# Loading most of the third group's k and v ahead of its transposable blocks on SP's queue

## The chip, the cores and the metric

The kernel runs on one core of a Trainium2 chip. The metric is the device time of one launch in microseconds (us), as the median over several runs. A core has a matrix engine (PE, with its weight loads shown apart as PEld), three engines for elementwise work (DVE, ACT, POOL), and a queue engine SP that does no arithmetic and only issues transfers. POOL issues transfers as well. All engines run their own instruction lists in order and wait for each other through semaphores.

## The reference, cut to what matters

Lightning attention over blocks of the sequence, with a decaying state per head, and then a two-layer network whose activation is h - tanh(h):

```python
# batch 4, heads 8, sequence 768, head size 64; lam: one decay per head
intra = einsum('bhic,bhjc->bhij', qb, kb) * Dmask        # scores within a block
intra = einsum('bhij,bhjd->bhid', intra, vb)
inter = einsum('bhid,bhde->bhie', qb * lam_pow, kv_state) # what came before the block
out   = intra + inter
kv_state = lam_block * kv_state + einsum('bhsd,bhse->bhde', kb * rev_pow, vb)
# bridge to x: 3072 tokens x 512
h = x @ w_in          # 512 x 2048
g = h - tanh(h)
y = g @ w_out         # 2048 x 512
```

## The kernel before, in words

**Tiling.** The sequence of 768 is cut into six groups of 128 positions (g = 0 to 5), and each group has one chunk for each of the four batches (b = 0 to 3). "The third group" is g = 2. Group 0 goes through a plain network (`up_plain`, `down_plain`), groups 1 to 5 through a network whose products are split by Strassen's scheme into seven (n = 1 to 7), and five of those seven are split once more into seven on the way down (`down_twice`, L536; x names the inner product). While the network of group g runs, the attention of group g + 1 is done in pieces between its products: `p0` for chunks 0 and 1, `p1` for chunks 2 and 3, each made of `att_transpose` (L275), `att_scores` (L296), `att_out` (L332) and `att_state` (L310).

**Two forms of the inputs.** For g of 2 and above (`GB = 2`) a chunk is loaded in two forms. The natural form, `k_nat` and `v_nat` (`load_natural`, L122, transfer at L127), has positions on partitions; one transfer of 256 KB each. `att_state` scales `k_nat` on DVE in place (L318) and multiplies it with `v_nat` on PE (L323); `att_out` multiplies `v_nat` with the scores on PE (L354). The block form, `q_blk` and `k_blk` (`load_blocks`, L132, transfers at L140), is sixteen transfers of 16 KB for each of q and k; DVE turns a block tile with one stream transpose into `qt` or `kt` (L283).

**Buffers.** `k_nat` has three buffers, `v_nat` four (L123, L124), used in turn by all groups. So k of chunk (2, 0) takes the buffer of (1, 1), k of (2, 1) that of (1, 2), k of (2, 2) that of (1, 3), and k of (2, 3) that of (2, 0); v of (2, b) takes that of (1, b). The buffers of group 1 come free with its `att_state`, one call for chunks 0 and 1 and one for chunks 2 and 3. The block tiles have seven buffers (L649), in memory that stages weights until `early.close()` (L648); the eighth block tile of a group, k of chunk 3, takes the buffer of the first and waits for its transpose.

**What sets the order.** All loads of the third group are issued by SP, in the order of `load` (L143 to L165), because `keep_in_program_order` holds the L127 and L140 transfers of g >= 2 to the order in which the program names them. Before the change that order is: blocks of q and k for chunks 0, 1, 2, the blocks of q for chunk 3 (seven tiles, 112 transfers), natural k and v of chunks 0 and 1, the k blocks of chunk 3, natural k and v of chunks 2 and 3. The same order is used for groups 3, 4 and (with v alone) 5. The main loop (L656 to L696) sets where the attention pieces stand among the products on PE: `down(g, 2)`, then `p0[2:]` (`att_out`, `att_state` of chunks 0 and 1), then `down_twice` with n = 4, the transposes of chunks 2 and 3 (`p1[0:1]`), `down_twice` with n = 5, the scores of chunks 2 and 3, and so on.

**Weights of the way down.** They lie in device memory (`factors`, `fine`) and come through a ring of seven buffers `wb` (`piece`, L472), loaded from POOL at L479 and L482. Results go out from POOL at L490.

Of the kernel before, what the change touches and what calls it, by code (L numbers as in the profile page):

```python
# [17 lines left out]
GB = 2  # L18
# [5 lines left out]
def kernel(  # L24
# [97 lines left out]
    def load_natural(g, b, names):  # L122
        for name, src, bufs in (("q", q, 2), ("v", v, 4), ("k", k, 3)) if (g, b) == (0, B - 1) else (  # L123
                ("q", q, 2), ("k", k, 3), ("v", v, 4)):  # L124
            if name in names:
                x = (qpool if name == "q" else io).tile([128, H, D], F32, name=f"{name}_nat", tag=name, bufs=bufs)
                op = nc.sync.dma_start(out=x, in_=src[b, :, ts(g, BLK), :].rearrange("h s d -> s h d"))  # L127
                if g >= GB:
                    tc.keep_in_program_order(op)
                raw[g, b][name] = x  # L130

    def load_blocks(g, b, names):  # L132
        for name, src in (("q", q), ("k", k)):
            if name in names:
                x = late["blk"].tile([128, NP, BLK // 32, 32], F32, name=f"{name}_blk", tag="blk")
                for p in range(NP):
                    for c in range(4):
                        blk = src[b, 2 * p + c // 2, ts(g, BLK), ts(c % 2, 32)]
                        tc.keep_in_program_order(
                            nc.sync.dma_start(out=x[ts(c, 32), p], in_=blk.rearrange("(r t) a -> t r a", t=32)))  # L140
                raw[g, b][name + "b"] = x

    def load(n):  # L143

        while at["loaded"] < min(n, len(chunks)):
            g, b = chunks[at["loaded"]]
            if g < GB:
                raw[g, b] = {}  # L150
                load_natural(g, b, "qkv")
                at["loaded"] += 1
                continue
            for b in range(B):
                raw[g, b] = {}
            nat = "kv" if g < NG - 1 else "v"
            for b in range(B - 1):
                load_blocks(g, b, "qk")
            load_blocks(g, 3, "q")
            for b in (0, 1):  # L160
                load_natural(g, b, nat)
            load_blocks(g, 3, "k")
            for b in (2, 3):
                load_natural(g, b, nat)
            at["loaded"] += B  # L165


# [93 lines left out]


    load(B)
    load_weights(WAHEAD)

# [9 lines left out]
    def att_transpose(g, bs):  # L275
        for b in bs:
            load(g * B + b + 1)
            t = raw[g, b]
            qt = work.tile([128, NP, BLK], F32, name="qt", tag="qt")
            kt = work.tile([128, NP, BLK], F32, name="kt", tag="kt")  # L280
            for dst, x in ((qt, "q"), (kt, "k")):
                if g >= GB:
                    tc.keep_in_program_order(nc.vector.transpose(out=dst.rearrange("d p i -> d (p i)"),  # L283
                                                                 in_=t[x + "b"].rearrange("d p r a -> d (p r a)")))
                else:
                    tp = bank("tp", "att", 4).rearrange("d (p s) -> d p s", p=NP)
                    for p in range(NP):
                        nc.tensor.transpose(out=tp[:, p, :], in_=t[x][:, 2 * p:2 * p + 2, :], identity=ident)
                    nc.scalar.activation(dst, tp, AF.Copy)
            qd = None  # L290
            if g > 0:
                qd = work.tile([128, NP, BLK], F32, name="qd", tag="qd")
                nc.vector.tensor_tensor(qd, qt, fwd, op=AL.mult)
            tr[g, b] = (qt, kt, qd)
# [432 lines left out]
```

## Time and profile before

| what | value |
|---|---|
| median of 4 runs | 690.72 us (686.94 to 694.71) |
| the profiled execution | 690.78 us, its span 689.0 us |
| PE busy | 665.7 us, 97% of the span |
| PEld, DVE, ACT, POOL busy | 575.9, 449.7, 194.3, 188.5 us |
| DMA | 123.27 MB, mean 179 GB/s |
| transfers of natural v, natural k (L127) | 24 and 20, 256 KB each, median 5.1 and 4.7 us to landing |
| transfers of blocks of q and of k (L140) | 256 and 256, 16 KB each, median 3.5 and 3.4 us to landing |
| `wb` from `fine`, from `factors` (POOL) | 168 and 44, 256 KB each, median 4.2 and 5.4 us to landing |

The span is the time from the first to the last recorded instruction of the one profiled execution; its own time is 1.78 us longer. A timeline row gives the start, the time, the engine and line, what is written and read, the number of instructions merged, and in brackets the idle time before it and what ended it. A row of stages gives the length of a stretch and each engine's busy time in it; PEclk is the share of full clock that PE was granted there.

### The profile page before, as it was taken

The numbers are of one execution on the slowest core, as the hardware profiler recorded it, in microseconds if no ns is written. First come the engines' busy times: TensorE is split into PE (matmuls) and PEld (weight loads), VectorE is DVE, ScalarE is ACT, GpSimd is POOL, SyncE is SP. The second block draws the span as 40 slices with busy tenths as digits, with TensorE's granted clock in tenths as the row PEclk, the third lists the DMA queues.
The fourth block names the chain that finished last, engine by engine and source line by source line (L and its number), as shares of the span: only waits on it lengthen the run. The fifth ranks groups of instructions, "written<-read, shape, count | busy, mean of one in ns | idle before, by whom it ended". The sixth has DMA issues, their size and how long they took to land.

```text
span 689.0 us, 12449 instructions
## 1 busy us (share of the span) xinstructions
PE 665.7 (97%) x4688; PEld 575.9 (84%) x4688; DVE 449.7 (65%) x786; ACT 194.3 (28%) x392; POOL 188.5 (27%) x325
## 2 busy tenths in 40 slices
PE   6899999999998789999999999999999999999998
PEld 5688855558887689888899888899988899988887
DVE  3798767992995775447885447777356776254743
ACT  2664433322321112332112332112233122233120
POOL 0001424227652245001254100144200244300352
PEclk9999999999999899999999999999999999999999
DMA  9869878639988898426498542498630576400485
GB/s 189 216 212 248 266 234 273 209 100 282 295 252 236 182 292 225 115 39 131 130 290 240 144 85 47 130 278 234 192 56 10 144 237 206 170 1 0 122 277 168
DMA packets 160427, 123.27 MB, mean 179 GB/s; under 512 B 133488, under 2 KB 133872, under 8 KB 160368
## 3 DMA queue, kind: packets, MB, share of 16 engines
q0 software_dynamic: 27504, 91.77, 41.9%
q1 hardware_dynamic: 132720, 30.71, 23.1%
q8 instruction: 37, 0.61, 0.4%
q14 instruction: 22, 0.18, 0.1%
q10 hardware_dynamic: 144, 0.00, 0.0%
HBM read 99.62 MB, written 22.81 MB: 178 GB/s over the span
## 4 chain that ended last, share of the span: by engine, by line
PE 87%; DMA 6%; issue 4%; POOL 2%; ACT 0%; DVE 0%; SPq 0%; POOLq 0%
PE y L405 20%; PE z L405 10%; PE y L548 10%; PE h L590 8%; PE op L606 8%; PE zw L548 7%; PE w L510 5%; PE w L405 5%; PE y L510 5%; PE sp L303 3%; DMA wb<-fine 3%; PE op L354 2%; POOL wb L479 1%; DMA wb<-factors 1%; PE op L348 1%
## 5 line engine op out<-in xcount | busy, mean ns | idle before, releaser
L479 POOL DMA_DIRECT2D wb<-fine x168 | 90.7, 540 | 143.1 <-PE y L548 56.9
L482 POOL DMA_DIRECT2D wb<-factors x44 | 24.0, 546 | 188.8 <-PE y L510 176.9
L405 PE MATMUL y<-xt,w 128*128 128x256 f32 x320 | 73.2, 379 | 0.0
L405 PEld LDWEIGHTS y<-xt,w 128*128 128x128 f32 x320 | 60.5, 190 | 8.5 <-issue 0.5
L413 ACT ACTIVATE th<-g 128x512 f32<-128x512 f32 x60 | 37.7, 630 | 93.1 <-DVE g L431 41.7
L551 ACT ACTIVATE q<-y 128x128 f32<-128x128 f32 x96 | 26.7, 278 | 124.0 <-PE y L548 123.1
L548 PE MATMUL y<-wb,g 128*128 128x128 f32 x456 | 61.3, 278 | 0.0
L414 DVE TENSOR_TENSOR g<-g,th 128x512 f32<-128x512 f32 x60 | 41.4, 689 | 27.5 <-ACT th L413 27.2
L548 PEld LDWEIGHTS y<-wb,g 128*128 128x128 f32 x456 | 55.7, 192 | 1.5 <-issue 0.3
L606 PE MATMUL op<-wt,g 128*128 128x512 f32 x128 | 56.5, 595 | 0.0
L590 PE MATMUL h<-xt,w 128*128 128x256 f32 x256 | 56.1, 381 | 0.0
L590 PEld LDWEIGHTS h<-xt,w 128*128 128x128 f32 x256 | 48.3, 190 | 7.3 <-issue 0.3
L606 PEld LDWEIGHTS op<-wt,g 128*128 128x128 f32 x128 | 23.8, 190 | 27.7 <-issue 26.5
L426 DVE TENSOR_TENSOR g<-g,z 128x512 f32<-128x512 f32 x20 | 13.7, 685 | 44.4 <-ACT g L425 44.4
L548 PE MATMUL zw<-wb,g 128*128 128x128 f32 x304 | 40.1, 275 | 0.0
L405 PE MATMUL z<-tt,ws 128*128 128x256 f32 x160 | 37.9, 380 | 0.0
L405 PE MATMUL y<-tt,w 128*128 128x256 f32 x160 | 37.9, 380 | 0.0
L405 PE MATMUL w<-xt,w 128*128 128x256 f32 x160 | 37.8, 379 | 0.0
L405 PE MATMUL y<-tt,ws 128*128 128x256 f32 x160 | 37.8, 379 | 0.0
L405 PE MATMUL z<-xt,ws 128*128 128x256 f32 x160 | 37.8, 379 | 0.0
L307 DVE TENSOR_TENSOR ss<-sp,mask 128x512 f32<-128x512 f32 x48 | 30.8, 682 | 10.7 <-PE sp L303 10.7
L548 PEld LDWEIGHTS zw<-wb,g 128*128 128x128 f32 x304 | 37.0, 192 | 0.0
(125 smaller groups left out, 1219.3 us busy)
## 6 DMA issues: line engine op xcount, KB each, us to landing
wb<-fine POOLq DMA_DIRECT2D x168, 256.0 KB, 4.2
wb<-factors POOLq DMA_DIRECT2D x44, 256.0 KB, 5.4
raw<-in_moe_w_out_dram POOLq DMA_DIRECT2D x16, 512.0 KB, 5.1
v_nat<-in_v_dram SPq DMA_DIRECT2D x24, 256.0 KB, 5.1
factors<-wt POOLq DMA_DIRECT2D x8, 768.0 KB, 5.5
k_nat<-in_k_dram SPq DMA_DIRECT2D x20, 256.0 KB, 4.7
raw<-in_moe_w_in_dram SPq DMA_DIRECT2D x8, 512.0 KB, 5.2
raw<-in_moe_w_in_dram SPq DMA_DIRECT2D x16, 256.0 KB, 5.1
```

Of the source, the lines that this page charges most:

```text
L303: nc.tensor.matmul(out=sp[j][:, p, :], lhsT=kt[ts(j, 64), p, :], rhs=qt[ts(j, 64), p, :], start=True, stop=True)
L307: nc.vector.tensor_tensor(ss[:, j], sp[j], mask[:, j], op=AL.mult)
L405: nc.tensor.matmul(out=t[:, m, :], lhsT=wt[:, kt, ts(m, 128)], rhs=x[:, kt, :], start=first and m == 0 and kt == 0, stop=kt == 1, skip_gro ...
L413: nc.scalar.activation(th, src, AF.Tanh)
L414: nc.vector.tensor_tensor(dst(c), src, th, op=AL.subtract)
L479: nc.gpsimd.dma_start(out=t.rearrange("p m c -> p (m c)"), in_=fine[TWICE.index(n_), SUB.index(x_)].rearrange("p u c -> p (u c)"))
L482: nc.gpsimd.dma_start(out=t, in_=factors[XAT[FACT[n_][1]]][:, 2 * x_:2 * x_ + 2, :])
L510: nc.tensor.matmul(out=t[:, m, :], lhsT=a[:, u, kt, ts(m, 128)], rhs=wb[:, kt, :], start=first and u == 0 and m == 0 and kt == 0, stop=u = ...
L548: nc.tensor.matmul(out=dst, lhsT=a[:, u, :], rhs=wb[:, ts(u, 128)], start=x in (1, 2) and u == 0, stop=u == NU - 1, skip_group_check=True)
L551: nc.scalar.activation(keep, dst, AF.Copy)
L590: nc.tensor.matmul(out=hm[:, m, :], lhsT=w1[u][:, i, a, ts(m, 128)], rhs=xt[0, t][:, i, :], start=m == 0 and i == 0, stop=i == KI - 1, ski ...
L606: nc.tensor.matmul(out=obank[b], lhsT=g, rhs=wt[:, 2 * a:2 * a + 2, :], start=kt == 0 and a == 0, stop=kt == KH - 1 and a == 1)
```

## The change

For the third group alone (g == GB), k and v of chunks 0, 1 and 2 in natural form are issued before any of the group's blocks. Their old places, before and after the k blocks of chunk 3, are left out for that group; natural k and v of chunk 3 stay behind those blocks. Six transfers move; none is added or taken away, and no other group changes.

```diff
@@ -154,14 +154,20 @@
             for b in range(B):
                 raw[g, b] = {}
             nat = "kv" if g < NG - 1 else "v"
+
+            first = (0, 1, 2) if g == GB else ()
+            for b in first:
+                load_natural(g, b, nat)
             for b in range(B - 1):
                 load_blocks(g, b, "qk")
             load_blocks(g, 3, "q")
             for b in (0, 1):
-                load_natural(g, b, nat)
+                if b not in first:
+                    load_natural(g, b, nat)
             load_blocks(g, 3, "k")
             for b in (2, 3):
-                load_natural(g, b, nat)
+                if b not in first:
+                    load_natural(g, b, nat)
             at["loaded"] += B
```

## The prediction

> **What bounds the kernel now.** I read the page first: PE is busy for 97% of the span, so time can be won only where PE stands idle. Then I asked for the waits, and for busy time by stage. The first three rows below run from the start of `att_out` of chunks 0 and 1 to the first product of `down_twice` n = 4, for g = 2, 3 and 4; the last three from there to the scores of chunks 2 and 3, for g = 2, 3 and 5. The work in each set is alike but for g = 5, which has no state to update.
>
> ```profile
> 220.20:232.96 12.76, 5.46 (x97) 4.77 (x97) 6.10 (x10) 1.09 (x2) 1.29 (x2) 0.73 0.75 153
> 337.36:341.22 3.86, 3.86 (x97) 3.62 (x97) 3.86 (x8) 1.08 (x2) 1.26 (x2) 1.00 0.41 136
> 443.19:447.05 3.86, 3.86 (x97) 3.62 (x96) 3.86 (x7) 1.09 (x2) 1.26 (x2) 1.00 0.34 127
> 232.96:248.01 15.05, 13.11 (x117) 12.80 (x114) 10.78 (x19) 2.50 (x9) 7.04 (x13) 1.00 0.97 263
> 341.22:353.92 12.70, 12.70 (x114) 12.58 (x114) 11.32 (x21) 2.50 (x9) 5.96 (x11) 1.00 1.03 282
> 553.00:565.70 12.70, 12.70 (x114) 12.58 (x114) 10.08 (x19) 3.19 (x11) 7.49 (x14) 1.00 0.76 243
> ```
>
> The third group loses 12.76 - 3.86 = 8.90 us in the first stretch and 15.05 - 12.70 = 2.35 us in the second. The timeline names what ends the first idle time:
>
> ```profile
> 223.44 0.39 SPq L127 DMA_DIRECT2D k_nat<-in_k_dram  x1
> 223.87 0.58 SPq L127 DMA_DIRECT2D v_nat<-in_v_dram  x1
> ...
> 226.55 5.61 SPq L140 DMA_DIRECT2D k_blk<-in_k_dram  x10
> 226.74 0.69 DVE L318 TENSOR_TENSOR k_nat<-k_nat,mask 128x512 f32<-128x512 f32 x1 [7.98 <-DMA k_nat<-in_k_dram]
> ...
> 227.94 1.98 PE L354 MATMUL op<-ss,v_nat 128*64 128x128 f32 x16 [6.64 <-DMA v_nat<-in_v_dram]
> ```
>
> SP reaches natural k and v of chunk 0 only at 223.44, when PE is already at `att_out`; DVE stands 7.98 us, PE 6.64. Why so late? SP's own timeline has it in 112 block transfers without a pause from 144.86 to 223.4. What it did before that, the waits of SP between 105 and 146 us say:
>
> ```profile
> SPq L127 <- PE kv L323: 18.9, 1, 18.9
> SPq L140 <- DMA raw<-in_moe_w_out_dram: 16.4, 2, 8.6
> SPq L140 <- DVE wt L260: 15.9, 1, 15.9
> ```
>
> After its last L127 transfer of group 1 (issued at 111.94) SP sat for some 32 us until the staging memory was free for the blocks: 16.4 + 15.9. That gap is where the six moved transfers go. The second stretch:
>
> ```profile
> 241.38 0.67 DVE L283 STREAM_TRANSPOSE kt<-k_blk 128x512 f32<-128x512 f32 x1
> ...
> 241.97 0.65 DVE L293 TENSOR_TENSOR qd<-qt,fwd 128x512 f32<-128x512 f32 x1
> 242.54 0.68 DVE L553 TENSOR_TENSOR gS<-gS,s 128x512 f32<-128x512 f32 x1
> 243.21 1.13 PE L548 MATMUL y<-wb,s 128*128 128x128 f32 x8 [1.94 <-DMA wb<-fine]
> ...
> 246.06 1.06 PE L548 MATMUL zw<-wb,gS 128*128 128x128 f32 x8
> ```
>
> PE waits 1.94 us for a weight piece, while SP's naturals of chunks 2 and 3 (235.17 to 239.4) share the DMA engines with it. The reader should also see the order on DVE: the transpose of chunk 3's k (241.38) stands ahead of L553, and L553 feeds the product at 246.06 (n = 5, x = 3).
>
> **What the Trainium skill says.** "DMA: Bandwidth & Descriptors", section "Anatomy of one DMA — SWDGE (gpsimd) path": a semaphore wait is served by the issuing sequencer before dispatch, not by the DMA engines. So a load that waits for its buffer holds everything behind it on SP; the trace agrees (18.9 us in one wait). Same page, "Issuing engines are not separate DMA queues": transfers of SP and POOL run on the same 16 engines, so moving one saves no transfer time; the trace agrees, the DMA share is 0.97 in the stretch where PE waits for `wb`. "TensorE: Matmul & The Clock Gate", "Part 1: The HAM clock gate": after an idle window of about 3.4 us PE falls to half clock. The trace agrees in kind: PEclk is 0.73 over the first stretch, against 1.00 in its like. That slow clock lies inside the 8.90 us; I don't add it.
>
> **The change, part by part.**
>
> *Moved to the front.* Natural k and v of chunk (2, 0) find their buffers free when `att_state` of group 1's chunks 0 and 1 ends (PE L323, 111.27 + 1.10 = 112.37): issued at about 112.4. Next is k of (2, 1), which must wait for k of (1, 2), read by the L323 that runs 139.86 to 140.96. Behind that wait on SP stand only v(2, 1), k and v(2, 2) and the blocks, and the blocks can't start before 144.8 in any case. Four naturals in a row took SP 226.44 - 223.44 = 3.0 us; from 140.5 or 141 they end by 144.0. So SP reaches the blocks on time.
>
> *Who else is disturbed.* k of (1, 3), issued at 111.94 and needed at 120.58, is ahead of the new pair on the queue; the weight loads of POOL at 112 and 114 share the engines with it. The waits between 105 and 150 us show no instruction waiting for `raw`; its users wait for PE. Cost 0 under that cover; without it, up to one landing, some 5 us.
>
> *Blocks pushed back.* The four naturals issued at 141 to 144 are still moving when the blocks begin. Bounds: 0 (the DMA share from 140 to 150 us is 0.49, so there is room for them) and 7.2 us (the four naturals of 223.44 took until 230.59, when their last consumer starts). I take d = 1 us: the blocks' 0.47 us each at the start is SP's own issue rate, and only the last natural or two are still out.
>
> *Removed from their old places.* Behind the seventh block tile (223.4 + d) SP goes straight to k blocks of chunk 3; the two pairs that stood before them took 3.0 us.
>
> *The stall.* Naturals in place since about 149, `att_out` and `att_state` run at 220.20 as for g = 3 and 4: -8.90 us. DVE's L318 no longer holds L532, L533 and L519, and POOL's store of L519 no longer holds the weight pieces (it waited 10.22 us).
>
> *What is late next.* Everything on PE and DVE shifts 8.90 us earlier, but SP's k blocks of chunk 3 shift only 3.0 - d = 2 us. DVE now wants them at 241.38 - 8.90 = 232.48. They are issued from 224.4; a tile's sixteen take 7.5 us at best (several rows), 8.53 here before, 10.5 at 201.43; I take 8.5 and a landing of 3.0 (medians by window: 2.0 to 5.0). Landing L = 223.4 + 1 + 8.5 + 3.0 = 235.9. From that transpose's start to the end of L553 is 242.54 + 0.68 - 241.38 = 1.84 us, with the hand-over 2.0: the product x = 3 starts at 237.9. Undisturbed it would start at 224.06 + 12.70 - 1.88 = 234.88 (1.88 is 247.94 - 246.06, from x = 3 to the scores). Loss 3.0 us. Bounds on L: 223.4 + 0 + 7.5 + 2.0 = 232.9 (loss 0), and 223.4 + 7.2 + 10.5 + 5.0 = 246.1 (loss 13.2, which is 2.0 us slower than before).
>
> *The weight wait.* Half of the naturals that shared its window are gone, and while PE waits for x = 3 the ring of seven fills: -2.35 us for the second stretch, in place of which stands the 3.0.
>
> *Later.* k and v of chunk (2, 3) follow at about 233 and land near 240; they are needed at 254.85 - 8.2. Group 3's blocks start some 5 us sooner; its naturals, issued at 308 to 311, are used at 337. So nothing downstream can undo the shift: PE is without a gap from 267 to 373.
>
> **Sum:** -8.90 - 2.35 + 3.0 = -8.2 us, against the profiled 690.78: 682.6. That execution is within 0.1 us of the median, so the same number stands for it. The four runs spread over 7.8 us.
>
> **The rivals.**
> 1. *Blocks in time.* L under 234, no new wait: the whole 11.25, 679.5 us. For it: the best block rate seen, 7.5 us. Against: weight pieces run at the same moment.
> 2. *Blocks later.* L of 239 to 242: x = 3 at 241 to 244, loss 6 to 9, 686 to 689. For it: block tiles took 10 to 13 us in the busy stretch from 164 to 223. Against: the two kinds of load met at 342.19 with 9.23 us a tile.
> 3. *Another wait in its place, or no move.* The weight ring, used 8.9 us sooner, waits as long as the naturals did, or the loads stay late because their buffer waits don't clear when I say: 689 to 691. Against: g = 3 and 5 run this stretch without a gap, g = 4 with 0.49 us.
> 4. *Slower.* Naturals and blocks pass one after the other: four landings of 4.9 us put the stream 19.6 us back, L = 254.5, x = 3 at 256.5, 10.4 us behind before: 701. It turns into a loss from L = 244.1 and reaches 1% at 251.0. Against: four naturals together took 7.2 us, not 19.6.
>
> **How the numbers follow.** One per cent is 6.9 us, about what a measurement can tell from no change; 683.8 corresponds to L = 237. Forecast (L from 234 to 238, 681 to 685): 0.55, of it 0.45 below 683.8. Rival 1: 0.12. Rival 2: 0.15. Rival 3: 0.08. Rival 4: 0.10. Faster 0.45 + 0.12 = 0.57; same 0.10 + 0.15 + 0.08 = 0.33; slower 0.10. The range from 678.5 to 690.0 takes in the forecast, rivals 1 and 2 and part of 3.
>
> **What would show it.** Right: L127 rows at about 112.4 and 140.5 to 144; blocks from about 145; no wait of L354 or L318 for a natural; the first stretch 3.9 us long; a DVE wait of about 3 us for `k_blk` before the last transpose, with x = 3 after it. Wrong: blocks starting after 147, a wait for `wb` over 2 us in `down_twice` n = 4 or 5, a PE gap before 155, or instructions of DVE in another order around the transposes.

## The result, and the profile after

The changed kernel takes 688.53 us (median of 43 runs, 684.70 to 691.55) against 690.8 us for the kernel before (64 runs): 0.9967 of its time, 95% interval 0.9956 to 0.9979. That is 2.3 us less, where 8.2 us less was forecast. Line numbers behind `load` are six higher from here on than in the kernel before: L289 is the stream transpose, L309 the scores, L324 the scaling of `k_nat`, L554 and L559 the products and the DVE step of `down_twice`.

The profiled execution (688.0 us span) has the two stretches of the forecast again, and a third from the product x = 3 of n = 5 to the first product of n = 6:

```profile
221.11:224.97 3.86, 3.86 (x97) 3.62 (x96) 3.86 (x7) 1.09 (x2) 1.29 (x2) 1.00 0.55 157
224.97:248.19 23.22, 14.94 (x117) 14.36 (x113) 11.76 (x21) 2.50 (x9) 7.04 (x13) 0.80 0.78 200
244.50:250.70 6.20, 6.20 (x49) 5.85 (x49) 3.21 (x7) 0.28 (x1) 1.08 (x2) 0.61 0.40 96
```

The first stretch is exactly what it is in the groups that never waited: 12.76 us became 3.86. The second grew from 15.05 to 23.22, and the clock column shows 0.80 in it and 0.61 in the third, which overlaps its end. The stall was handed on. The timeline of DVE and PE says to whom:

```profile
235.37 1.06 PE L554 MATMUL y<-wb,gS 128*128 128x128 f32 x8
...
242.51 0.71 DVE L289 STREAM_TRANSPOSE kt<-k_blk 128x512 f32<-128x512 f32 x1 [8.84 <-DMA k_nat<-in_k_dram]
243.15 0.65 DVE L299 TENSOR_TENSOR qd<-qt,fwd 128x512 f32<-128x512 f32 x1
243.72 0.68 DVE L559 TENSOR_TENSOR gS<-gS,s 128x512 f32<-128x512 f32 x1
...
244.50 2.05 PE L554 MATMUL zw<-wb,gS 128*128 128x128 f32 x8 [8.08 <-issue]
246.34 1.91 PE L554 MATMUL y<-wb,gS 128*128 128x128 f32 x8
248.19 2.58 PE L309 MATMUL sp<-qt,kt 64*128 64x128 f32 x32
```

DVE stands 8.84 us before the transpose of chunk 3's k. L559 is two places behind it, and the product that starts at 244.50 needs L559; PE stands 8.08 us. A row of eight like instructions took 1.06 us at 235.37 and 2.05 us after the pause. "issue" in PE's bracket means that the profile names no releaser; the times of L559 give it. SP's timeline shows why the blocks came so late:

```profile
141.16 0.37 SPq L127 DMA_DIRECT2D k_nat<-in_k_dram  x1
141.58 1.68 SPq L127 DMA_DIRECT2D v_nat<-in_v_dram  x1
143.43 1.91 SPq L127 DMA_DIRECT2D k_nat<-in_k_dram  x1
145.38 2.15 SPq L127 DMA_DIRECT2D v_nat<-in_v_dram  x1
147.91 7.99 SPq L140 DMA_DIRECT2D q_blk<-in_q_dram  x16
...
219.65 8.99 SPq L140 DMA_DIRECT2D q_blk<-in_q_dram  x16
228.75 9.85 SPq L140 DMA_DIRECT2D k_blk<-in_k_dram  x16
238.89 0.38 SPq L127 DMA_DIRECT2D k_nat<-in_k_dram  x1
```

The naturals go out when forecast, at 141, but the issue of the last four holds SP for 6.4 us (141.16 to 147.53), not 3.0. The blocks start at 147.91 instead of 144.86, and the last k block is issued at 238.6.

### The profile page after: what moved, and what is told of

The parts are those of the page before. It is cut to its first block, busy times and chain, and to the rows that moved or that the text cites. A ratio compares the mean times of both kernels' runs of the same rounds, so it can differ in the third digit from the quotient of the medians.

```text
span 688.0 us, 12453 instructions
## 1 busy us (share of the span) xinstructions
PE 666.7 (97%) x4688; PEld 577.1 (84%) x4688; DVE 449.9 (65%) x786; ACT 194.5 (28%) x392; POOL 188.7 (27%) x325
## 4 chain that ended last, share of the span: by engine, by line
PE 87%; DMA 5%; issue 3%; DVE 2%; POOL 1%; SPq 1%; ACT 0%; POOLq 0%; DVEq 0%
PE y L411 20%; PE y L554 11%; PE z L411 10%; PE zw L554 8%; PE op L612 8%; PE h L596 6%; PE w L516 5%; PE w L411 5%; PE y L516 5%; PE sp L309 3%; PE op L360 2%; DMA raw<-in_moe_w_in_dram 2%; DMA wb<-fine 2%; DMA wb<-factors 1%; PE op L354 1%
## 5 line engine op out<-in xcount | busy, mean ns | idle before, releaser
L554 PE MATMUL y<-wb,g 128*128 128x128 f32 x456 | 61.3, 278 | 0.0
L554 PEld LDWEIGHTS y<-wb,g 128*128 128x128 f32 x456 | 55.7, 192 | 1.5 <-issue 0.3
L554 PE MATMUL zw<-wb,g 128*128 128x128 f32 x304 | 40.2, 275 | 0.0
L554 PEld LDWEIGHTS zw<-wb,g 128*128 128x128 f32 x304 | 37.0, 192 | 0.0
```

Of the source, the lines that this page charges most:

```text
L554: nc.tensor.matmul(out=dst, lhsT=a[:, u, :], rhs=wb[:, ts(u, 128)], start=x in (1, 2) and u == 0, stop=u == NU - 1, skip_group_check=True)
```

## The experiments

Each ratio is to the kernel before, timed alongside. **The theory:** the moved loads remove the wait at `att_out`, but push back the block stream on SP; chunk 3's k blocks then hold L559 on DVE and with it PE. **The rivals:** PE would have waited there for weight pieces anyway; the gain was lost elsewhere; or that one execution was a chance.

**1. The changed kernel once more**, no edit.

> The changed kernel once more, for a second profile. Theory (the stall was handed on: the k blocks of chunk 3 land late, the stream transpose waits on DVE, L559 behind it feeds the product x = 3 of n = 5): the stretch from the first product of n = 4 to the scores of chunks 2 and 3 is 20 to 24 us again where it could be 12.70, with the wait before the last transpose at 6 to 9 us and x = 3 starting 2.0 us after the blocks' landing; 0.997 of the time before. Rival (a chance of that one execution): the wait is under 3 us here and PE's idle time is elsewhere.

687.45 us, 0.9959 (0.9945 to 0.9972). Its timeline, and its stage from x = 3 to n = 6:

```profile
239.68 0.71 DVE L289 STREAM_TRANSPOSE kt<-k_blk 128x512 f32<-128x512 f32 x1 [6.19 <-DMA k_nat<-in_k_dram]
...
241.67 2.05 PE L554 MATMUL zw<-wb,gS 128*128 128x128 f32 x8 [5.69 <-issue]
```

```profile
241.67:248.29 6.62, 6.62 (x49) 6.28 (x49) 3.24 (x7) 0.28 (x1) 1.08 (x2) 0.57 0.52 113
```

The same wait again, 2.65 us shorter (8.84 - 6.19), and x = 3 again 2.0 us behind it. The second stretch is 245.35 - 224.78 = 20.57 us. The size of the wait differs between executions, its place doesn't.

**2. No k blocks for chunk 3.** Sixteen transfers are left out; the transpose reads chunk 2's tile.

```diff
-            load_blocks(g, 3, "k")
+            if g == GB:
+                raw[g, 3]["kb"] = raw[g, 2]["kb"]
+            else:
+                load_blocks(g, 3, "k")
```

> Leaves out the sixteen k block transfers of chunk 3 of the third group; its transpose reads the block tile of chunk 2 instead, so the values of that chunk are not the reference's. Theory: without that landing the stretch from n = 4 to the scores is 12.7 to 13.5 us, and the whole is 9 to 11 us below the time before, 680 to 682 us. Rival (the weight ring is as late as the blocks, since POOL and SP share the DMA engines): PE then waits in the same stretch for wb, 4 us or more, and the time is 685 to 688.

680.64 us, 0.9865 (0.9834 to 0.9896). On its timeline the transpose starts without a wait:

```profile
232.11 0.70 DVE L292 STREAM_TRANSPOSE qt<-q_blk 128x512 f32<-128x512 f32 x1
...
232.73 0.67 DVE L292 STREAM_TRANSPOSE kt<-k_blk 128x512 f32<-128x512 f32 x1
234.44 1.16 PE L557 MATMUL zw<-wb,s 128*128 128x128 f32 x8 [1.12 <-DMA wb<-fine]
```

The total is what the theory gave, the stretch is not: 15.04 us (224.11 to 239.15) where 12.7 to 13.5 was expected. PE waits for weight pieces there, 1.12 and 0.70 us. So the rival holds in kind but not in size, for it asked for 4 us or more: with the blocks in time, weights are the next wait, far smaller than the 5.7 to 8.1 us taken away. The missing transfers also let SP start the next group's blocks sooner (229.09), into the same stretch.

**3. Two chunks ahead instead of three.**

```diff
-            first = (0, 1, 2) if g == GB else ()
+            first = (0, 1) if g == GB else ()
```

> Only chunks 0 and 1 ahead, so two natural transfers less stand between the free buffers (141 us) and the blocks. Theory (the naturals push the block stream back): the blocks start 1 to 2 us sooner than at 147.9, the k blocks of chunk 3 land at 238 to 240 instead of 242.4, and the time is 2 to 4 us below that of the changed kernel, 685 to 687. Rival (the stream's end is set by the load of the DMA engines between 156 and 228 us, whatever its start): landing within 1 us of the changed kernel's, same time.

684.97 us, 0.9925 (0.9894 to 0.9955). SP, and the transpose:

```profile
145.88 7.55 SPq L140 DMA_DIRECT2D q_blk<-in_q_dram  x16
...
224.56 8.85 SPq L140 DMA_DIRECT2D k_blk<-in_k_dram  x16
```

```profile
238.28 0.71 DVE L289 STREAM_TRANSPOSE kt<-k_blk 128x512 f32<-128x512 f32 x1 [4.64 <-DMA k_nat<-in_k_dram]
...
240.26 2.05 PE L554 MATMUL zw<-wb,gS 128*128 128x128 f32 x8 [4.33 <-issue]
```

Two transfers fewer ahead start the stream 2.0 us sooner than in the changed kernel, and the wait ends 4.2 us sooner than in its profile (1.4 sooner than in the second one). As executions of one kernel differ by as much, the other profiles matter: in the five with three chunks ahead where this transpose waits, it starts 18.8 to 21.4 us after `att_out`; here it starts 17.2 us after it. The rival, that the stream's end doesn't depend on its start, falls: the seven tiles take 78.7 us here (145.88 to 224.56), 78.6 before, 80.8 and 78.2 in the two profiles of the changed kernel, and 77.7 to 80.9 in the seven others that issue all these loads from SP. A later start is not made good on the way. The time is 2.5 us below experiment 1's; the two intervals overlap a little.

**4. Chunk 3 handled later.** Its transposes go behind n = 6 and its scores behind n = 7; `att_out` and `att_state` of chunks 2 and 3 follow the first product of the next group's way up (`up`). All transfers are as in the changed kernel.

```diff
-        run(p1[0:1])                      # before n = 5
+        split = g + 1 == GB
+        run([(att_transpose, g + 1, (2,))] if split else p1[0:1])
...
-        run(p1[1:2])                      # before n = 6
+        run([(att_scores, g + 1, (2,))] if split else p1[1:2])
...
-        run(p1[2:])                       # before n = 7
+        run([(att_transpose, g + 1, (3,))] if split else p1[2:])
         down_twice(g, 7, "w")
+        if split:
+            att_scores(g + 1, (3,))
         if not last:
             up(g + 1, 0, 1)
+            if split:
+                run(p1[2:])
```

> The changed kernel with the transposes of chunk 3 of the third group taken from before n = 5 to after n = 6, and its scores, att_out and att_state from before n = 6 and n = 7 to after n = 7; all transfers as in the changed kernel. Theory (only the place of the transpose ahead of L559 on DVE costs): no wait for k_blk, the stretch from n = 4 to the scores of chunk 2 is about 12 us with half the scores in it, 680 to 682 us in all, with at most 1 to 2 us given back where att_out follows the late scores. Rival (weights late): PE waits for wb instead, 686 or more.

680.56 us, 0.9856 (0.9828 to 0.9885).

```profile
233.58 0.69 DVE L559 TENSOR_TENSOR gS<-gS,s 128x512 f32<-128x512 f32 x1 [0.27 <-PE zw L554]
...
238.25 1.16 PE L309 MATMUL sp<-qt,kt 64*128 64x128 f32 x16
...
245.06 0.70 DVE L289 STREAM_TRANSPOSE kt<-k_blk 128x512 f32<-128x512 f32 x1
```

L559 no longer stands behind the transpose, and by 245.06 the blocks are there; from n = 4 to the scores of chunk 2 it takes 238.25 - 225.24 = 13.01 us. The transfers, the late blocks among them, are the changed kernel's. So it was not their lateness as such that cost the time, but what stood behind their consumer on DVE. This version beats both kernels.

**5. Only the later place**, on the kernel before: the edit of 4 without the change.

> The kernel before, with all natural loads in their old places, and only the transposes, scores, att_out and att_state of chunk 3 moved back as in e4_late_chunk3. Theory (the later place is worth something only once the natural loads are early): the wait of PE for v_nat at att_out of chunks 0 and 1 stays, about 8.9 us lost there, so within 3 us of the time before. Rival (the later place is a gain by itself, since chunk 3 is done late): 6 us or more below the time before.

691.00 us, 1.0015 (0.9997 to 1.0033): no gain.

```profile
226.92 1.97 PE L354 MATMUL op<-ss,v_nat 128*64 128x128 f32 x16 [5.59 <-DMA v_nat<-in_v_dram]
...
243.81 1.55 PE L548 MATMUL zw<-wb,s 128*128 128x128 f32 x8 [2.40 <-DMA wb<-fine]
245.15 1.91 PE L548 MATMUL y<-wb,gS 128*128 128x128 f32 x8
```

Most of the old wait for `v_nat` is there: 5.59 us against 6.64, and the first stretch takes 11.69 us (220.22 to 231.91) against 12.76. With 4, the four kernels make a square: neither edit, 1; the early loads alone, 0.9967; the later place alone, 1.0015; both, 0.9856. The two edits need each other.

**6. Which load is it?** The profile names `k_nat` as the releaser of the wait. Here chunk 3's natural k is not loaded; its state update uses chunk 2's tile.

```diff
+                    if g == GB:
+                        load_natural(g, b, "v")
+                        raw[g, b]["k"] = raw[g, 2]["k"]
```

> The changed kernel without the natural k load of chunk 3 of the third group; its state update uses chunk 2's tile, scaled twice, so its values are not the reference's. The trace of the changed kernel names k_nat as what ended the wait of the last transpose. Theory (it is the last k block transfer that lands there): the wait before that transpose stays at 4 to 9 us and the time within 2 us of the changed kernel's. Rival (the transpose, through a shared semaphore, waits for k_nat): the wait vanishes, 680 to 682 us.

688.50 us, 0.9975 (0.9955 to 0.9995).

```profile
233.16 0.71 DVE L293 STREAM_TRANSPOSE qt<-q_blk 128x512 f32<-128x512 f32 x1 [1.59 <-DMA k_blk<-in_k_dram]
240.63 0.71 DVE L293 STREAM_TRANSPOSE kt<-k_blk 128x512 f32<-128x512 f32 x1 [6.75 <-DMA k_blk<-in_k_dram]
```

The wait stays and is now put down to `k_blk`. The name in the other profiles was that of a later transfer.

**7. Is the slow clock a cost of its own?** Products without use fill the pause.

```diff
+            if (g, n, x) == (1, 5, 3):
+                warm = bank("warm", "att", 4)
+                for _ in range(14):
+                    tc.keep_in_program_order(nc.tensor.matmul(
+                        out=warm, lhsT=ident, rhs=mask[:, 0].rearrange("s p i -> s (p i)"), start=True, stop=True))
```

> The changed kernel with 14 products of 128x512 added on PE just before the product x = 3 of n = 5, their result not used, some 6 us of work at the 0.44 us a piece of the down_plain products, inside the pause for the k blocks. Theory (a pause this long brings PE to half clock, which costs 2.3 to 2.8 us after it): PEclk stays 1.00 over the pause, from x = 3 to the first product of n = 6 it takes 3.9 us instead of 6.2 to 6.6, and the time is 1.5 to 2.5 us below the changed kernel's. Rival (the slow products after the pause have another cause): that stretch still takes over 6 us, or the extra work shows as a longer time.

690.16 us, 1.0015 (1.0001 to 1.003): the time expected did not come. One product is two instructions of 0.44 us, so the 14 outlasted the wait:

```profile
235.01 12.18 PE L556 MATMUL warm<-mask,ident 128*128 128x512 f32 x28
...
241.53 0.68 DVE L564 TENSOR_TENSOR gS<-gS,s 128x512 f32<-128x512 f32 x1
...
247.03 1.05 PE L559 MATMUL zw<-wb,gS 128*128 128x128 f32 x8
```

L564 was done at 242.21, and x = 3 began 4.8 us later. With `range(7)`:

> e7_warm with 7 products instead of 14: each turned out to take 0.87 us there, so that the 14 outlasted the wait by some 5 us. Theory (half clock after the pause costs 2.3 to 2.8 us): 7 products fill 6.1 us of the pause, PEclk stays 1.00, x = 3 to the first product of n = 6 takes 3.9 us, and the time is 1.5 to 2.5 us below the changed kernel's, ratio to before 0.992 to 0.994. Rival (no clock cost): ratio 0.996 to 0.997, as the changed kernel's.

684.73 us, 0.9940 (0.9919 to 0.9962). The filled pause and the stretch after it:

```profile
234.63:240.64 6.01, 6.01 (x16) 2.66 (x15) 2.23 (x4) 0.28 (x1) 0.62 (x2) 1.00 0.99 261
240.64:244.50 3.86, 3.86 (x49) 3.62 (x47) 2.87 (x7) 0.28 (x1) 1.07 (x2) 1.00 0.37 87
```

PEclk is 1.00 throughout, and 3.86 us stand against 6.20 and 6.62 in the two profiles of the changed kernel. So the clock is a cost of its own, of 2.3 to 2.8 us in this stretch. In the whole it shows less surely: 0.9940 is 1.3 to 1.9 us below 0.9959 and 0.9967, but its interval overlaps both of theirs.

**8. Two chunks ahead and the later place** (3 and 4 together).

> e4_late_chunk3 with only chunks 0 and 1 ahead of the blocks. Theory: nothing waits for the blocks any more in either, so it equals e4_late_chunk3 within 1 us, 680 to 682. Rival (the block stream's start still matters): 1 to 2 us below e4_late_chunk3.

680.74 us, 0.9875 (0.9847 to 0.9903). As the theory has it: once nothing stands behind the late blocks, their landing doesn't matter. The rival's further gain isn't there.

**9. Four naturals from ACT's queue.**

```diff
+                eng = nc.scalar if g == GB and b in (1, 2) else nc.sync
-                op = nc.sync.dma_start(out=x, ...)
+                op = eng.dma_start(out=x, ...)
```

> The changed kernel with the natural k and v of chunks 1 and 2 of the third group issued from ACT's queue; by the compiled order they stand on ACT between the tanh of the network's last part before att_out, at about 190 us. Theory (the wait and the issue of these four on SP delay the block stream by some 3 us): the blocks start at 144.9 to 145.5, those of chunk 3's k land 2 to 3 us sooner than with the changed kernel, 685 to 686 us. Rival (the stream is paced by the shared DMA engines, whoever issues): its start is early but it takes longer, the landing is within 1 us of the changed kernel's, and so is the time.

687.74 us, 0.9977 (0.9957 to 0.9996), inconclusive as a time. SP's blocks, and ACT:

```profile
143.84 7.45 SPq L141 DMA_DIRECT2D q_blk<-in_q_dram  x16
```

```profile
200.32 0.37 ACTq L128 DMA_DIRECT2D k_nat<-in_k_dram  x1
203.93 0.37 ACTq L128 DMA_DIRECT2D v_nat<-in_v_dram  x1
204.41 0.63 ACT L420 ACTIVATE th<-g 128x512 f32<-128x512 f32 x1 [9.97 <-DMA q_blk<-in_q_dram]
...
241.85 2.01 PE L555 MATMUL y<-wb,gS 128*128 128x128 f32 x8 [1.28 <-DMA wb<-fine]
```

This execution runs 1.66 us ahead by then (its first moved load goes out at 110.91, the changed kernel's at 112.57), so the stream's start is 2.4 us sooner, as expected, and no transpose waits. But ACT stood 9.97 us among its loads, a tanh came late, and PE reached `att_out` only at 225.81. One block tile held SP for 21.01 us (from 185.81), so that the seven took 81.1. One wait was exchanged for another; the edit doesn't isolate the stream.

## Why the prediction was wrong

**The chain of causes was right; sizes in it were wrong, and one term was missing.** The loads went into SP's gap at 112 and 141; the stall of `att_out` went in full (8.90 us); what came late next was the transpose of chunk 3's k, and x = 3 followed its start by 1.99 us in both profiles (forecast 2.0). The forecast's "blocks later" rival describes the outcome; it was given 0.15.

**The step that failed is "Blocks pushed back", d = 1 us, and with it the landing L = 235.9 and the loss of 3.0 us under "What is late next".** Measured from the start of `att_out`, L was forecast at 235.9 - 220.20 = 15.7 us. It was 242.51 - 221.11 = 21.4 in the profile and 239.68 - 220.92 = 18.8 in the second. The terms, for both:

| term | forecast | profile | second |
|---|---|---|---|
| end of the seventh tile, from `att_out`'s start | 4.2 | 7.6 | 5.6 |
| issue of the last tile's sixteen | 8.5 | 9.85 | 8.9 |
| last issue to landing | 3.0 | 3.9 | 4.3 |

The first row holds d, the push on the block stream. Before the change the seventh tile ended 3.2 us after the start of `att_out` (223.44 - 220.20), so d was 4.4 us in the profile and 2.3 in the second (5.57 - 3.24), not 1. In the profile this is the largest miss; in the second the landing missed by as much (1.3 us).

Two readings behind d failed. The first is that four naturals hold SP for 3.0 us, so that "SP reaches the blocks on time": the 3.0 was read at 223.44, where the DMA share was 0.69, but now they held SP for 6.4 us and, in the second profile, 7.1 (140.87 to 147.93). The blocks began at 147.91 and 148.29, and "blocks starting after 147" was the forecast's own sign of being wrong. The second is the DMA share of 0.49 between 140 and 150 us, a mean over 0.73 in its first half and 0.24 in the other. The naturals run at the seam; from 141 to 148 the row of the kernel before is

```profile
141.00:148.00 7.00, 7.00 (x17) 3.17 (x18) 7.00 (x14) 0.00 (x0) 1.43 (x2) 1.00 0.62 190
```

and of the changed kernel

```profile
141.00:148.00 7.00, 7.00 (x36) 3.40 (x32) 7.00 (x14) 0.35 (x1) 2.07 (x3) 1.00 0.97 263
```

Four naturals came on top of POOL's weight stores and filled it. The forecast bounded d by 7.2 and then took a value near the lower end.

**A term was missing.** The half clock was seen in the old stall and not charged to the new one. In the kernel before, the stretch from x = 3 to n = 6 is

```profile
246.06:249.93 3.87, 3.87 (x51) 3.63 (x49) 2.56 (x6) 0.56 (x2) 1.63 (x4) 1.00 1.10 307
```

After pauses of 8.1 and 5.7 us it cost 6.20 - 3.87 = 2.3 and 6.62 - 3.87 = 2.8 us more. Experiment 7 shows this cost by taking it away. The Trainium skill ("TensorE: Matmul & The Clock Gate", "Part 1: The HAM clock gate") puts the loss of clock at an idle window of about 3.4 us. The traces agree in that 4.33 us of idle PE (two chunks ahead) were followed by products of 2.05 us instead of 1.06. They differ in that shorter pauses were followed by slow products too: 2.40 us in experiment 5 (1.91) and 1.28 us in experiment 9 (2.01; PEclk 0.51 from 241.85 to 244.00), while the 1.94 us of the kernel before were not (1.13). So it is open whether the forecast wait of 3.0 us would have cost the clock.

**The sum with measured terms.** x = 3 would stand 14.68 us after `att_out`'s start if nothing waited (234.88 - 220.20). It stood at 244.50 - 221.11 = 23.39 in the profile, a loss of 8.7, and 241.67 - 220.92 = 20.75 in the second, 6.1. With the clock 11.0 and 8.8, against a gain of 8.90 + 2.35 = 11.25: net 0.2 and 2.4 us. The medians give 2.3 and 2.6 (690.01 - 687.45), but the sum does not explain them to the tenth. As a whole the two executions took 1.0 and 3.5 us less than the profiled one before. Their third group began 0.9 and 0.7 us late (0.6 of the 0.9 already at 100 us, ahead of the change), and they won another 1.8 and 1.9 us after 574 us, where the kernel before waits 1.57 us for a weight piece (660.64). With two chunks ahead PE waits 1.11 us near that place (656.94), so this late gain is not shown to be the change's doing.

**The weight wait** of 2.35 us was taken as gone. In the changed kernel it lies under the pause and can't be judged. With the pause gone it is partly there: the stretch takes 15.04 us without the k blocks, and 13.01 and 13.07 with the later place (experiments 4 and 8), against 12.70 undisturbed. Without the k blocks the next group's blocks run in it too, so these three don't settle it.

**What stays open:** why the landing differs by some 3 us between executions of one kernel, and whether the naturals slow SP by their own descriptors or by POOL's traffic; experiment 9 was to tell and didn't.

## What to carry to other kernels

In these runs, loads moved to the front of an in-order queue delayed everything behind them, and the stream, some 80 us long, did not make the delay good: find the last consumer of such a stream, and see what else stands behind it on its engine. Moving loads early and moving the late load's consumer back can each be worth almost nothing alone and 1.4% together. When a wait is moved, price it again with everything that hung on the old one, the clock included, and read the load of the DMA engines over the exact microseconds in which the moved transfers will run.

## What the runs showed of the hardware

Filling an idle PE with 7 products that nobody reads kept PEclk at 1.00 and brought the stretch after the pause from 6.20 and 6.62 us to 3.86; the whole took 0.9940 of the time before. A short pause can be followed by slow products, and not by its length alone: a row of eight took 2.01 us after a pause of 1.28 us (with one of 0.53 us shortly before it), and 1.13 us after one of 1.94 us.

Four loads of 256 KB held SP for 3.0 us at a DMA share of 0.69, and for 6.4 and 7.1 us at 0.97 and 0.99. And a transfer named as the releaser of a wait need not be the one waited for: without the named load the wait was still 6.75 us.
